# Sliding-window attention beside a long convolution on one core: logits and softmax in two halves, paired 64-row tails, and a fixed VectorE order at the end

## Chip, core and metric

The kernel runs on one core of a Trainium2 chip. The metric is the device time of one execution in microseconds (us); less is better. TensorE multiplies, VectorE and ScalarE work elementwise, GpSimd builds tables, and the queues of SyncE (SP), ScalarE and GpSimd start transfers, which 16 DMA engines carry out.

## What is computed

Two blocks that do not depend on each other, written side by side into the output (S = 2048, D = 576, bfloat16):

```python
# block A: 32 heads of 18, each token looks at itself and at 7 tokens before it, two apart
q, k, v = split(x @ wqkv)
idx = pos[:, None] - 2 * arange(8)[None, :]           # mask: idx >= 0
logits = einsum("bhsd,bhswd->bhsw", q, k[idx]) * 18 ** -0.5
a = einsum("bhsw,bhswd->bhsd", softmax(where(mask, logits, -1e9)), v[idx]) @ wo
# block B: a 4-tap shift convolution, a gate, and a causal convolution over the whole sequence
kv = (sum of k_pad[:, t:t + S] * shift_k[:, 3 - t] over 4 taps) * v_B
y = irfft(rfft(kv, 2 S) * rfft(ssm_k, 2 S))[:S]       # per channel
b = q_B * (y + kv * ssm_D)
out = concatenate([a, b], -1)
```

## The kernel before

*Block A.* x is transposed into xT by 80 TensorE transposes (L146); the rows 512 to 576 of the contraction are held as a fifth block of 128 rows whose first half is zero. From xT come q and k (qk_step L248, qk_half_step L260; steps of 128 channels by 1,024 tokens) and v (v_step L235). wv is held with its columns permuted from (head, d) to (d, head); permute_wv (L309) does this on ScalarE, after a load into a scratch area. logit_step, one for each of the 8 window positions, multiplies q and shifted k on VectorE (L395, L403) and adds the 18 products of a head by a matmul with a 0/1 matrix (L398, L407), into Lsb. Only when all 8 are there can the softmax begin: softmax_a (maximum, subtraction, exponential) and softmax_b (sum, reciprocal, product), each in two halves of columns, then at_step transposes the weights. pv_step(tp), for two of the 16 values of t mod 16, forms P = v x weights on VectorE (L547), adds over the window by matmuls with the identity (L556), and multiplies by wo (L569).

*Block B.* The long convolution is a two-step Fourier transform by matmuls, with its intermediate results in DRAM: x_step (shift convolution of kv_step on VectorE, L342 to L348, then the first transform s1_chunk, L279) writes Dx; k_step (transposes L293, then s1_chunk) writes Dk. kh_step does the second transform s2 (L454) of the filter into Khat; g_step does s2 for x, multiplies the spectra on VectorE (L491 to L494), does the inverse of the second transform (L500) and writes Dy; y_step does the last transform (L586), multiplies by q_B (L587) and stores.

*Order.* The program is written as a sequence of steps, and `run(a, b)` mixes two lists of them in proportion: q and k steps with x and k steps; logits with kh and v steps; then softmax, v 12 to 15, the copy of v's window rows (halo), g 0 and 1; then pv steps with g and y steps. A scheduler places the instructions of a step on the engines by priority, which follows the written order; each engine then runs its own queue in order. Two pools of two PSUM buffers each, pa (psA) and pb (psB), pass results to ScalarE and VectorE, and the input and Wt loads, the stores and the intermediate transfers go through SP's queue.

Of the kernel before, what the change touches and what calls it, by code (L numbers as in the profile page):

```python
# [18 lines left out]
def kernel(  # L19
# [114 lines left out]
    nc.gpsimd.memset(wq[0:64, 4, :], 0.0)  # L134
    nc.gpsimd.memset(wv[0:64, 4, :], 0.0)


    for qtr in range(4):
# [100 lines left out]
    def wcols(kb, comp, ct):  # L239
        return wq[:, kb, comp * D + 128 * ct:comp * D + min(128 * ct + 128, D)]  # L240

    def qk_step(comp, ct, jp):
        pad = PADL if comp else 0
        ps = psa()
        for u in range(2):
            j = 2 * jp + u
            for kb in range(5):
                nc.tensor.matmul(ps[:, u, :], wcols(kb, comp, ct), xT[:, kb, 512 * j:512 * j + 512],  # L248
                                 start=(kb == 0), stop=(kb == 4))
        dest = (k2 if comp else q2)[ct // 2][:, ct % 2, pad + 1024 * jp:pad + 1024 * jp + 1024]  # L250
# [376 lines left out]
```

## Time and profile before

| | |
|---|---|
| median of 3 timed runs | 293.98 us (292.49 to 295.75) |
| the profiled execution | 296.45 us, of which the span of the trace 294.6 us |
| busy: TensorE, weight loads | 241.2 us (82%), 152.6 us |
| busy: VectorE, ScalarE, GpSimd | 201.3 us (68%), 167.5 us (57%), 25.9 us (9%) |
| moved by DMA | 52.37 MB, mean 178 GB/s |
| mean granted TensorE clock | 0.905 of 2.4 GHz |

Busy times are of one execution. Weight loads run beside matmuls. A group's row gives its busy time, the mean of one instruction, and the idle time of the engine just before it with what ended that idle time. The chain of waits is followed back from the last instruction; each piece says what ran or what was waited for. A TensorE instruction's own duration holds its latency too, so the pitch of a row of matmuls is read from a piece of the chain, length over count.

### The profile page before, as it was taken

What the parts mean: (1) busy time and instruction counts of PE and PEld (TensorE: products, weight loads), DVE (VectorE), ACT (ScalarE), POOL (GpSimd) and SP (SyncE); (2) the same over time, 40 slices, a digit from 0 to 9 for tenths busy, and PEclk for the clock granted to TensorE, in tenths of its full rate; (3) what the DMA queues carried; (4) which work ended last, traced back from release to release, by engine and by line L of the source; (5) the groups of instructions that cost most, each with busy time, mean ns of one, the idle gap of its engine ahead of it and who ended that gap; (6) DMA issues with size and microseconds to landing.
All of it is one profiled execution on the core that took longest, in us unless ns stands there. A gap on an engine that the chain in (4) does not pass through costs nothing.

```text
span 294.6 us, 5101 instructions
## 1 busy us (share of the span) xinstructions
PE 241.2 (82%) x2129; PEld 152.6 (52%) x2129; DVE 201.3 (68%) x188; ACT 167.5 (57%) x242; POOL 25.9 (9%) x60
## 2 busy tenths in 40 slices
PE   1579269999997779999999455379999999997993
PEld 1464024555543336565547233168676766766782
DVE  3750895898771149899977991685879669694531
ACT  2422656668868662877877957323576585550311
POOL 8200000000000000000000845000000000012200
PEclk9999859999999778999999857558999999998999
DMA  7999623595555556653344198820442432559982
GB/s 232 360 323 305 234 77 144 178 285 163 160 162 160 160 160 184 222 148 94 103 148 145 40 278 221 283 82 0 123 146 110 149 127 94 184 154 309 328 255 80
DMA packets 42594, 52.37 MB, mean 178 GB/s; under 512 B 2174, under 2 KB 36686, under 8 KB 42445
## 3 DMA queue, kind: packets, MB, share of 16 engines
q1 hardware_dynamic: 39644, 47.04, 50.4%
q0 software_dynamic: 1264, 3.17, 4.3%
q10 hardware_dynamic: 1664, 1.84, 1.9%
q8 instruction: 16, 0.26, 0.3%
q14 instruction: 6, 0.05, 0.0%
HBM read 31.11 MB, written 18.87 MB: 170 GB/s over the span
## 4 chain that ended last, share of the span: by engine, by line
PE 50%; ACT 17%; DMA 16%; DVE 11%; issue 5%; SPq 1%; DVEq 0%; ACTq 0%
PE psA L248 9%; PE psA L235 7%; PE psB L279 6%; PE psA L556 5%; PE psB L454 5%; PE psA L569 5%; DMA out_dram<-m 4%; DMA xnat<-in_A_x_dram 4%; ACT Xc L457 4%; DMA Dy<-Y 4%; DMA k<-in_A_wqkv_dram 4%; PE psB L293 3%; PE psA L398 3%; ACT Y L503 3%; ACT vst L283 3%
## 5 line engine op out<-in xcount | busy, mean ns | idle before, releaser
L248 PE MATMUL psA<-xT,wq 128*128 128x512 bf16 x160 | 42.7, 407 | 8.7 <-ACT q L251 8.1
L556 PE MATMUL psA<-ident,P 128*128 128x128 bf16 (+1 forms) x640 | 46.2, 231 | 1.5 <-DVE P L547 1.4
L556 PEld LDWEIGHTS <-P 128*128 128x128 bf16 (+1 forms) x640 | 40.9, 107 | 8.4 <-issue 4.6
L547 DVE TENSOR_TENSOR P<-vX,at 128x4608 bf16<-128x4608 bf16 x16 | 40.1, 2550 | 4.3 <-PE psA L556 4.3
L283 ACT ACTIVATE vst<-psB 128x768 bf16<-128x768 f32 x48 | 36.3, 814 | 9.1 <-PE psB L279 8.0
L395 DVE TENSOR_TENSOR prod<-q,k 128x4096 bf16<-128x4096 bf16 x16 | 36.1, 2284 | 0.8 <-PE psA L398 0.6
L248 PEld LDWEIGHTS <-wq 128*128 128x128 bf16 x160 | 16.2, 103 | 27.8 <-issue 14.1
L454 PE MATMUL psB<-Wt,W 128*64 128x288 bf16 x256 | 28.0, 312 | 1.5 <-ACT Y L503 0.6
L560 ACT ACTIVATE xT<-psA 128x1024 bf16<-128x1024 f32 x8 | 8.2, 1024 | 34.8 <-PE psA L556 34.8
L500 PE MATMUL psB<-m,IAt 64*128 64x288 bf16 x128 | 14.9, 320 | 14.2 <-DVE m L493 7.6
L235 PE MATMUL psA<-wv,xT 128*128 128x288 bf16 x160 | 25.3, 294 | 0.3 <-ACT vX L237 0.3
L491 DVE TENSOR_TENSOR m<-Xc,Khat 128x2304 bf16<-128x2304 bf16 x8 | 10.8, 1356 | 18.6 <-ACT Xc L457 18.6
L503 ACT ACTIVATE Y<-psB 128x576 bf16<-128x576 f32 x32 | 18.9, 650 | 7.4 <-PE psB L500 6.1
L296 DVE COPY kTt<-psB 128x1152 bf16<-128x1152 bf16 x8 | 6.1, 758 | 24.0 <-PE psB L293 23.9
L569 PE MATMUL psA<-wv,xT 128*128 128x288 bf16 x160 | 22.3, 287 | 0.0
L235 PEld LDWEIGHTS <-xT 128*128 128x128 bf16 x160 | 18.8, 147 | 6.8 <-issue 6.8
L539 POOL DMA_DIRECT2D wv<-in_A_wo_dram x18 | 8.9, 501 | 151.7 <-PE psA L235 146.2
L457 ACT ACTIVATE Khat<-psB 128x576 bf16<-128x576 f32 x32 | 19.5, 653 | 3.4 <-PE psB L454 3.1
L587 DVE TENSOR_TENSOR m<-psB,Lsb 128x576 bf16<-128x576 f32 x16 | 11.4, 752 | 14.6 <-DMA out_dram<-m 8.2
L457 ACT ACTIVATE Xc<-psB 128x576 bf16<-128x576 f32 x32 | 19.6, 651 | 1.3 <-PE psB L454 1.1
L454 PEld LDWEIGHTS <-W 128*64 128x64 bf16 x256 | 12.7, 112 | 13.5 <-issue 11.9
L146 PE MATMUL psA<-ident,xnat 128*128 128x128 bf16 x80 | 9.5, 310 | 11.1 <-DMA xnat<-in_A_x_dram 10.0
(116 smaller groups left out, 331.2 us busy)
## 6 DMA issues: line engine op xcount, KB each, us to landing
Dx<-vst SPq DMA_DIRECT2D x16, 288.0 KB, 3.0
Dk<-vst SPq DMA_DIRECT2D x16, 288.0 KB, 3.0
Wt<-Dk SPq DMA_DIRECT2D x8, 576.0 KB, 3.8
Wt<-Dx SPq DMA_DIRECT2D x8, 576.0 KB, 3.9
Dy<-Y SPq DMA_DIRECT2D x8, 576.0 KB, 3.0
Wt<-Dy SPq DMA_DIRECT2D x8, 576.0 KB, 6.0
kX<-in_B_k_dram SPq DMA_DIRECT2D x3, 1008.0 KB, 5.2
vt<-in_B_v_dram SPq DMA_DIRECT2D x4, 576.0 KB, 8.3
```

The source lines that it names most:

```text
L235: nc.tensor.matmul(ps[:, di, 0:288], xTt[:, kb, t2, :], wv[:, kb, d0:d1], start=(kb == 0), stop=(kb == 4))
L248: nc.tensor.matmul(ps[:, u, :], wcols(kb, comp, ct), xT[:, kb, 512 * j:512 * j + 512], start=(kb == 0), stop=(kb == 4))
L279: nc.tensor.matmul(ps[:, ri, 0:384], T1[:, ri, :], sf[:, 384 * ch:384 * ch + 384], start=True, stop=not extra)
L283: nc.scalar.activation(vst[:, :, 384 * ch:384 * ch + 384], ps[:, :, 0:384], ACT.Copy)
L395: nc.vector.tensor_tensor(prod[:], q2[ct // 2][:], k2[ct // 2][:, :, sh:sh + S], ALU.mult)
L454: nc.tensor.matmul(ps[64 * hp:64 * hp + 64, im, 0:HD], W2[:, im, 8 * g + 2 * prl + hp].rearrange("p l f -> p (l f)"), Wt[:, 2 * prl + hp, ...
L457: nc.scalar.activation(dst[:, :, prl, :], ps[:, :, 0:HD], ACT.Copy, scale=scale)
L500: nc.tensor.matmul(ps[:, hp, 0:HD], IAt[64 * hp:64 * hp + 64, zi, 4 * g + prl, :], m1[64 * hp:64 * hp + 64, zi, prl, :], start=(zi == 0), ...
L503: nc.scalar.activation(Y[:, 2 * prl:2 * prl + 2, :], ps[:, :, 0:HD], ACT.Copy)
L547: nc.vector.tensor_tensor(P[:].rearrange("p w (d h) -> p w d h", h=H), vs, at[:, :, t2, :].unsqueeze(2).to_broadcast([128, W, DH, H]), ALU ...
L556: nc.tensor.matmul(oacc[0:csz, ci, 128 * u:128 * u + 128], Ps[u][:, wi, 128 * ct:128 * ct + csz], ident[:], start=(ci % 2 == 0 and u == 0 ...
L569: nc.tensor.matmul(pso[:, di, 0:288], oT[:, ct, t2, :], wot[:, ct, d0:d1], start=(ct == 0), stop=(ct == 4))
```

## The change

1. **Halves of t mod 16.** Logits are formed for t mod 16 below 8 first (all 8 window positions), then for the rest: `logit_unit(hf, wi)`. Each has its own tile Lh[hf], its own softmax and its own transposed weights ath[hf]. Half 0's softmax stands among the logit units of half 1. Each product has half the columns of before, in runs of 8 elements.
2. **Moved work.** q and k steps are by 512 tokens and begin when the first quarter of x is transposed. The first transforms of x alone stand beside them; those of the filter, all v steps and the halo (now in four parts) stand beside the logits; kh steps 4 to 7 stand in the last stage. The table transposes (ia_tables) come early.
3. **Loads.** x, weights, k and v of block B all go through SP, x 0 first, then the q and k weights, x 1, the first k and v block, x 2, x 3. B_shift_k is loaded once as one row and spread over the partitions by a matmul. wv is loaded without permutation; v's eviction permutes.
4. **Paired tails.** The rows 512 to 576 of xT, of the weights and of oT are held twice (both halves of 128 partitions), and their 64-row matmuls are issued in pairs for the two halves of the array; the last 64 columns of P are summed for two t in two column halves.
5. **Fixed VectorE order in the last stage.** `pin` makes each P product and each spectral product follow the one before it in the written order; `plan` says which k, g and y steps go with which tp. The second transform of g + 1 is issued ahead of the product of g.
6. **Memory.** Pools on the other sides, slabs of `cv` shared by several uses (tA: convolution, Lh, q_B; vt: v_B, ath; tB: convolution, sums, Y; wide: k_B and products).

```diff
-            for kb in range(5):
-                nc.tensor.matmul(ps[:, di, 0:288], xTt[:, kb, t2, :], wv[:, kb, d0:d1],
-                                 start=(kb == 0), stop=(kb == 4))
-        nc.scalar.activation(vX[:, 14 + t2, :].rearrange("p (i d) -> p i d", i=2), ps[:, :, 0:288], ACT.Copy)
+            for kb in range(4):
+                nc.tensor.matmul(ps[:, di, 0:288], xTt[:, kb, t2, :], wv[:, kb, d0:d1], start=(kb == 0), stop=False)
+        for di, (d0, d1) in enumerate(DCH):
+            r = slice(64 * di, 64 * di + 64)
+            nc.tensor.matmul(ps[:, di, 0:288], xTt[r, 4, t2, :], wv[r, 4, d0:d1], start=False, stop=True,
+                             tile_position=(64 * di, 0))
+        nc.scalar.activation(vX[:, 14 + t2, :].rearrange("p (d i h) -> p d i h", i=2, h=16),
+                             ps[:, :, 0:288].rearrange("p i (h d) -> p d i h", d=DH), ACT.Copy)
...
+                prod = wide().rearrange("p (c t) -> p c t", c=2)[:, :, 0:1024].rearrange("p c (a b) -> p c a b", b=8)
+                qv = q2[h][:].rearrange("p c (a b) -> p c a b", b=NT)[:, :, :, 8 * hf:8 * hf + 8]
+                kv = k2[h][:, :, sh:sh + S].rearrange("p c (a b) -> p c a b", b=NT)[:, :, :, 8 * hf:8 * hf + 8]
+                nc.vector.tensor_tensor(prod, qv, kv, ALU.mult)
+                for c in range(2):
+                    for j in range(4):
+                        nc.tensor.matmul(psw[32 * j:32 * j + 32, u, 0:256].rearrange("p (a b) -> p a b", b=2),
+                                         Eh[:, 2 * h + c, :], prod[:, c, :, 2 * j:2 * j + 2],
+                                         start=(h == 0 and c == 0), stop=False, tile_position=(0, 32 * j))
...
+    units = [logit_unit(hf, wi) for hf in range(2) for wi in range(W)]
+    for n, un in enumerate(units):
+        run(un, fill[3 * n:3 * n + 3] + vh[n * 20 // 13:(n + 1) * 20 // 13])
+        with tc.high_priority():
+            if n == 9:
+                softmax_a(0)
+            if n == 10:
+                softmax_b(0)
+            if n == 12:
+                at_step(0)
...
+        if n >= 12:
+            kh_step(n - 12)
+    with tc.high_priority():
+        softmax_a(1)
+        softmax_b(1)
+        at_step(1)
...
+    plan = [(("k4", "g0"), ("k5", "g1")), (("k6", "g2"),), (("k7", "g3"), ("g4",)), (("g5",), ("y0",)),
+            (("g6",), ("y1",), ("y2",)), (("g7",), ("y3",)), (("y4",), ("y5",)), (("y6",), ("y7",))]
+    g_spec(0)
+    for tp in range(8):
+        pv_mul(tp)
...
+        for n, i in enumerate(ng):
+            if i + 1 < 8:
+                g_spec(i + 1)
+            if n == 0:
+                pv_sum(tp)
+            g_prod(i)
+            if n == 0 and tp > 0:
+                pv_out(tp - 1)
+            g_inv(i)
```

Three places show how instructions move. The first is ScalarE's queue at the second and third q and k steps, where before the copies that permute wv stand (k_1 there is the scratch area that the weights were loaded into). Before:

```order
L251 ACTIVATE q_0_286<-psA 128x1024
L251 ACTIVATE k_0_288<-psA 128x1024
L309 ACTIVATE wv<-k_1_289 128x576 x4
L309 ACTIVATE wv<-k_1_289 64x576
L251 ACTIVATE q_0_286<-psA 128x1024
```

Now, the same queue from the last piece of B_shift_k (sk) through the first quarter's q and k steps to the second quarter of xT:

```order
L361 ACTIVATE sk<-psB 128x4x64
L283 ACTIVATE q_0_87<-psA 128x2x512
L283 ACTIVATE k_0_89<-psA 128x2x512
L283 ACTIVATE q_1_88<-psA 128x2x512
L283 ACTIVATE k_1_90<-psA 128x2x512
L181 ACTIVATE xT<-psA 128x2x512
L283 ACTIVATE q_0_87<-psA 128x2x512
```

The four copies of wv and the fifth of 64 rows are gone from between the q and k evictions, and nothing of the v weights stands in their place.

The second place is VectorE's queue at the second half's softmax (before: the only one). Lsb are the logits, mx the maxima and sums, m a spectral product. Before, from the subtraction of the maximum on:

```order
L422 TENSOR_TENSOR Lsb<-Lsb,mx 128x8x256 x2
L491 TENSOR_TENSOR m_1688<-Xc,Khat 128x2304
L492 TENSOR_TENSOR m_1689<-Xc,Khat 128x2304
L493 TENSOR_TENSOR m_1688<-m_1688,m_1689 128x1152
L494 TENSOR_TENSOR m_1688<-m_1688,m_1689 128x1152
L428 TENSOR_TENSOR mx_1771<-Lsb 128x1024
L428 TENSOR_TENSOR mx_1781<-Lsb 128x1024
L429 TENSOR_TENSOR mx_1771<-mx_1771 128x512
L429 TENSOR_TENSOR mx_1781<-mx_1781 128x512
L431 TENSOR_TENSOR ssum<-mx_1771 128x256
L431 TENSOR_TENSOR ssum<-mx_1781 128x256
L433 RECIPROCAL rec<-ssum 128x256 x2
```

Now, where tA is half 1's logits, tB its maxima and sums, and vt the transposed weights ath:

```order
L493 TENSOR_TENSOR tA<-tA,tB 128x2048
L640 TENSOR_TENSOR P<-vX,vt 128x4608
L500 TENSOR_TENSOR tB<-tA 128x1024
L640 TENSOR_TENSOR P<-vX,vt 128x4608
L501 TENSOR_TENSOR tB<-tB 128x512
L568 TENSOR_TENSOR m_2131<-Xc,Kc 128x2304
L503 TENSOR_TENSOR tB<-tB 128x256
L569 TENSOR_TENSOR sk<-Xc,Kc 128x2304
L505 RECIPROCAL tB<-tB 128x256
L570 TENSOR_TENSOR m_2131<-m_2131,sk 128x1152
L507 CAST tB<-tB 128x256
L571 TENSOR_TENSOR m_2131<-m_2131,sk 128x1152
```

Before, a single spectral product stood inside the softmax and every P behind it; now the first two P, which need half 0 alone, stand between the two passes of half 1's softmax, and the first spectral product is threaded through the second. TensorE's transposes of half 1 stand ahead of all sums over P in its queue.

The third place is VectorE's queue in the last stage, with the waits, where output steps (L690, into m) and the last spectral product (L568 to L571) alternate:

```order
L640 TENSOR_TENSOR P<-vX,vt 128x4608
L640 TENSOR_TENSOR P<-vX,vt 128x4608 [waits PE_49]
L690 TENSOR_TENSOR m_3049<-psB,tA 128x576 [waits DMAHW7_49,DMASW6_49,PE_49]
L690 TENSOR_TENSOR m_3049<-psB,tA 128x576 [waits PE_49]
L690 TENSOR_TENSOR m_3067<-psB,tA 128x576 [waits DMASW7_49,DVE_49,PE_49]
L690 TENSOR_TENSOR m_3067<-psB,tA 128x576 [waits PE_49]
L568 TENSOR_TENSOR m_3169<-Xc,Kc 128x2304 [waits DMAHW3_49,DVE_49,Activation_49]
L569 TENSOR_TENSOR sk<-Xc,Kc 128x2304
```

Before, all output steps stood behind the last spectral product, five of them in a row behind the fifteenth P; now they are spread among products and P from tp 3 on, and both kinds share the two buffers m, so the last spectral product waits for a store (DMAHW).

## Rows read from the trace of the kernel before

**Rows 1.** Busy time by stage: PE, PEld, DVE, ACT, POOL (instructions); PEclk, DMA share, GB/s.
```profile
0.00:21.20 21.20, 9.53 (x81) 8.41 (x82) 11.76 (x33) 7.03 (x7) 8.75 (x32) 1.00 0.93 306
21.20:39.30 18.10, 10.06 (x40) 4.22 (x40) 8.78 (x7) 9.01 (x9) 0.00 (x0) 0.86 0.74 233
39.30:110.00 70.70, 65.38 (x343) 31.66 (x343) 43.32 (x37) 49.42 (x63) 0.00 (x0) 0.91 0.55 172
110.00:158.50 48.50, 47.69 (x496) 27.73 (x494) 42.88 (x34) 32.66 (x56) 0.00 (x0) 0.97 0.48 147
158.50:190.40 31.90, 17.19 (x135) 11.53 (x134) 23.42 (x30) 21.84 (x33) 13.44 (x23) 0.69 0.72 206
190.40:202.10 11.70, 9.81 (x90) 8.15 (x90) 7.44 (x4) 2.92 (x5) 0.00 (x0) 0.53 0.13 53
202.10:259.80 57.70, 54.65 (x672) 39.16 (x669) 47.02 (x31) 37.07 (x61) 0.00 (x0) 1.00 0.36 119
259.80:294.60 34.80, 26.91 (x282) 21.75 (x280) 16.70 (x19) 7.50 (x12) 3.74 (x5) 0.93 0.78 238
sum 294.60, PE 241.21 PEld 152.61 DVE 201.32 ACT 167.47 POOL 25.93; mean PE 30.15 PEld 19.08 DVE 25.16 ACT 20.93 POOL 3.24
```

**Rows 2.** Chain of waits: start us, length us, what, xcount.
```profile
21.05 11.16 DMA k<-in_A_wqkv_dram
...
52.15 2.26 PE psA L248 x10
...
92.17 1.17 PE psB L293 x10
...
129.76 2.12 PE psA L235 x16
...
132.45 0.61 PE psB L454 x8
...
133.46 0.57 PE psA L398 x8
...
195.43 7.11 PE psA L556 x72
...
207.78 2.80 PE psA L556 x48
```

**Rows 3.** VectorE groups by shape: busy us, mean ns | idle before, releasers.
```profile
L547 DVE TENSOR_TENSOR P<-vX,at 128x4608 bf16<-128x4608 bf16 x16 | 40.1, 2550 | 4.3 <-PE psA L556 4.3
...
L395 DVE TENSOR_TENSOR prod<-q,k 128x4096 bf16<-128x4096 bf16 x16 | 36.1, 2284 | 0.8 <-PE psA L398 0.6
...
L347 DVE TENSOR_TENSOR tA<-tA,tB 128x2304 bf16<-128x2304 bf16 x12 | 16.3, 1356 | 0.3
...
L587 DVE TENSOR_TENSOR m<-psB,Lsb 128x576 bf16<-128x576 f32 x16 | 11.4, 752 | 14.6 <-DMA out_dram<-m 8.2 <-PE psB L586 6.3
...
L491 DVE TENSOR_TENSOR m<-Xc,Khat 128x2304 bf16<-128x2304 bf16 x8 | 10.8, 1356 | 18.6 <-ACT Xc L457 18.6
...
L493 DVE TENSOR_TENSOR m<-m,m 128x1152 bf16<-128x1152 bf16 x8 | 6.1, 758 | 0.3
...
L433 DVE RECIPROCAL rec<-ssum 128x256 f32<-128x256 f32 x2 | 3.4, 1718 | 0.0
...
L422 DVE TENSOR_TENSOR Lsb<-Lsb,mx 128x2048 bf16<-128x2048 bf16 x2 | 2.4, 1218 | 0.0
```

**Rows 4.** Groups by shape on TensorE (L248) and ScalarE.
```profile
L248 PE MATMUL psA<-xT,wq 128*128 128x512 bf16 x160 | 42.7, 407 | 8.7 <-ACT q L251 8.1 <-ACT xT L149 0.6
...
L283 ACT ACTIVATE vst<-psB 128x768 bf16<-128x768 f32 x48 | 36.3, 814 | 9.1 <-PE psB L279 8.0 <-ACT kh L269 0.8
...
L237 ACT ACTIVATE vX<-psA 128x576 bf16<-128x576 f32 x16 | 10.4, 651 | 6.6 <-PE psA L235 6.6
...
L309 ACT ACTIVATE wv<-k 128x576 bf16<-128x576 bf16 x4 | 4.7, 1254 | 4.1 <-DMA k<-in_A_wqkv_dram 4.1
```

**Rows 5.** DMA issues: what, queue, count, size of one, us to landing.
```profile
out_dram<-m SPq DMA_DIRECT2D x8, 288.0 KB, 5.2
```

More of the change, by code (lines that the diff above doesn't have):

```diff
@@ L133, with x_tr @@
     nc.vector.tensor_copy(ident[:], ident_f[:])
[L134 to L138 removed]
+    def x_tr(qtr):
+        nc.vector.tensor_copy(xns[qtr][:, :, D:640], xns[qtr][:, :, 512:D])
         for kp in range(3):
@@ L256, in qk_half_step @@
         for j in range(2):
-            for kb in range(5):
+            for kb in range(4):
                 for hh in range(2):
@@ new lines, in qk_steps, with sk_step @@
+    def qk_steps(j):
+        return [lambda comp=comp, cp=cp: qk_step(comp, cp, j) for cp in range(2) for comp in range(2)]
+    skb = slab("sk", 1, (4, D), "skb")
+    ones1 = tw.tile([1, 128], BF16, name="ones1")
+    nc.gpsimd.memset(ones1[:], 1.0)
+    def sk_step():
+        for i in range(3):
+            n = 256 if i < 2 else 64
+            ps = psb()
+            for u in range(2 if i < 2 else 1):
+                m = 512 if i < 2 else 256
+                nc.tensor.matmul(ps[:, u, 0:m], ones1[:], shr[:, 1024 * i + 512 * u:1024 * i + 512 * u + m],
+                                 start=True, stop=True)
+            nc.scalar.activation(skb[:, :, 256 * i:256 * i + n],
+                                 ps[:].rearrange("p u (d j) -> p j (u d)", j=4)[:, :, 0:n], ACT.Copy)
@@ new lines, in x_part @@
+    def x_part(c2, ch):
+        if c2 % 2 == 0 and ch == 0:
+            kvt[0] = kv_conv(c2 // 2)
+        s1_part(kvt[0][:, 2 * (c2 % 2):2 * (c2 % 2) + 2, :], "x", c2, ch, Dx, False)
+    x_tr(0)
+    sk_step()
+    for f in qk_steps(0):
+        f()
+    ia_tables()
+    x_tr(1)
+    kvl[1] = load_kv(1)
+    nc.sync.dma_start(wv[:, 0:4, :], A_wqkv[0:512, 2 * D:3 * D].rearrange("(kb p) a -> p kb a", p=128))
+    for p0 in (0, 64):
+        nc.sync.dma_start(wv[p0:p0 + 64, 4, :], A_wqkv[512:576, 2 * D:3 * D])
@@ new lines, with k_tr @@
+    for f in qk_steps(1):
+        f()
+    x_tr(2)
+    x_tr(3)
+    tw.release()
+    xin.release()
+    kpre = pool("kpre", 1, "right")
+    knats = []
+    for db in range(5):
+        n = 128 if db < 4 else 64
+        kn = kpre.tile([128, S], BF16, name=f"knat{db}")
+        nc.sync.dma_start(kn[0:n, :], B_ssm_k[128 * db:128 * db + n, :])
+        knats.append(kn)
+    nc.gpsimd.dma_start(Db[:], B_ssm_D.partition_broadcast(128))
+    ktt = {}
+    def k_tr(c2):
+        ktt[c2] = kpre.tile([128, 2, D], BF16, name="kTt", bufs=3)
+        ptr = pb.tile([128, 2, 1024], BF16, name="psB")
+        for u in range(2):
+            for db in range(5):
+                n = 128 if db < 4 else 64
+                nc.tensor.transpose(ptr[:, u, 128 * db:128 * db + n],
+                                    knats[db][0:n, :].rearrange("p (a b) -> p b a", b=NT)[:, 2 * c2 + u, :],
+                                    ident[0:n, 0:n])
+        nc.vector.tensor_copy(ktt[c2][:], ptr[:, :, 0:D])
@@ new lines, in k_part, with xs, ks, ld @@
+    def k_part(c2, ch):
+        if ch == 0 and c2 == 0:
+            k_tr(0)
+            k_tr(1)
+        if ch == 0 and c2 + 2 < 8:
+            k_tr(c2 + 2)
+        s1_part(ktt[c2], "k", c2, ch, Dk, True)
+    def xs(c2s):
+        return [lambda c2=c2, ch=ch: x_part(c2, ch) for c2 in c2s for ch in range(3)]
+    def ks(c2s):
+        return [lambda c2=c2, ch=ch: k_part(c2, ch) for c2 in c2s for ch in range(3)]
+    def ld(c):
+        def f():
+            kvl[c] = load_kv(c)
+        return f
```

532 lines of the change are left out of this document (265 added, 267 removed).

## Prediction

> **What bounds the kernel now.** I read the busy windows first: one row per stage, with each engine's busy time and TensorE's granted clock [rows 1]. The reader should see three kinds of stretch. Up to 21.2 us the DMA engines are the limit (share 0.93) and TensorE works 9.5 us. From 39.3 to 158.5 and from 202.1 to 259.8 TensorE is busy over 90% of the time. In between lie two holes. From 21.2 to 39.3 TensorE works 10.1 of 18.1 us: the chain of waits runs through an 11.16 us load of the v weights [rows 2], behind which ScalarE reorders them in four copies of 1.25 us and a fifth of 64 rows [rows 4]; the next eviction of q stands behind these copies in ScalarE's queue, and the group of the q and k matmuls lost 8.1 us for it [rows 4]. From 158.5 to 202.1 everything waits for the softmax: TensorE is busy 27 of 43.6 us at a clock of 0.69 and then 0.53, so the first 72 sums over P take 7.11 us where 48 later ones take 2.80 (0.099 and 0.058 us each) [rows 1, 2]. At the end, from 259.8, TensorE is busy 26.9 of 34.8 us, and VectorE waits 8.2 us for output stores before it may refill their buffers [rows 3].
>
> No engine is near its sum: VectorE has 201.3 us of work, ScalarE 167.5 [rows 1]. TensorE's 241.2 are partly stretched by the clock. At the pitches of undisturbed chain pieces (128x512: 0.226; 128x288: 0.1325; 128x128 sums: 0.058 [rows 2]) I get about 208 us. So the question is whether the change closes the holes, and at what price in work.
>
> **Prices of the edits.** *Paired tails.* Eight matmuls of the two-at-a-time form take 0.61 us [rows 2], where four times 0.1325 is 0.53; eight of the four-at-a-time form with 512 columns take 0.57, where twice 0.226 is 0.45. So members of a group do run beside each other, and entering and leaving such a group costs 0.08 to 0.12 us; I use 0.1. A pair of 512-column tails then costs 0.33 instead of 0.45 (16 pairs, -2.0 us), a v pair 0.23 instead of 0.265 (16, -0.5), four tails of the output product 0.365 instead of 0.53 (8, -1.3), sixteen 64-row sums 0.57 instead of 0.93 (8, -2.9): -6.7 us together. Row-halved pairs of 512 columns are not in the trace; between no overlap (+1.6 us) and full overlap without a switch (-3.6) I take the rows of the nearest paired form. [...] *Logits by halves.* Before, 16 groups of eight (0.57) and 8 of eight with 256 columns (0.35 by the same rule): 11.9 us. After, 32 groups at 0.35 and 16 with 128 columns at 0.23: 14.9, +3.0. *B_shift_k by matmul*: five of 512 columns, +1.1. TensorE's sum thus hardly moves (-2.6).
>
> *VectorE.* A product of 4,096 elements takes 2.284 us, one of 2,048 takes 1.218 [rows 3]: 32 x 1.218 - 36.1 = +2.9. The small products go from 5.5 to 16 x 0.43 = +1.4 (0.51 ns per element, from the 1,152 and 2,048 rows). Four new copies of 256 elements, +1.2; the copy of skb goes, -1.4. Sum +4.1. The new products read runs of 8 elements, which the trace lacks: bounds are 1.218 and, at the 1 ns per element of the PSUM product (0.752 for 576 [rows 3]), 2.3. I take the lower end, since P's product, in runs of 32 with a broadcast operand, keeps 0.55 ns per element.
>
> *ScalarE.* The permutation (6.0) goes into v's eviction, which costs between 0.65 as now and 1.25 as the permuting copy did [rows 4]: 0 to +9.6 us over 16. I take the upper end, its nearest row. Sixteen steps share the logits stage with TensorE, which hides them (below).
>
> So no work disappears. The gain must come from where the waits go.
>
> **Stage 1, to the end of the shift convolutions.** x leaves SP's queue ahead of everything, and the first k, v pair stands behind the q and k weights and a second x block: 0.6 + 1.5 + 0.6 + 1.6 = 4.3 MB, at 306 GB/s [rows 1] 14 us plus some 2 to issue. New on VectorE: the copy that doubles x's tail stands ahead of the identity and the tables, so these wait for x; I allow 2 us, hidden since the k, v data come later anyway. The convolutions start near 17 us; the load and copy of skb that they waited for are gone. VectorE then runs 32 operations of 1.356 us (43.4 [rows 3]), x and table copies (some 8), two early products (2.4): end near 71. TensorE has 128 x 0.226 + 16 x 0.33 for q and k, 80 + 34 transposes at 0.117 [rows 2], some 11 of others: 59 us from about 6, with some 6 of waits for x and its copies, and ends beside it. Its last six column blocks of Dx wait for convolution 3: ScalarE evicts them at 0.81 each [rows 4], so stage 2 is under way at 75.
>
> **Stage 2, logits.** TensorE: v 16 x 1.29 = 20.6; the transforms of B_ssm_k, moved here, 8 x 1.17 [rows 2] + 24 x 0.35 = 17.8; logits 14.9; four steps of kh 16 x 0.365 = 5.8; transposes 1.9: 61.0 us. VectorE: 30 products and 16 small ones 43.4, kTt 8 x 0.76 = 6.1, softmax of half 0 some 7.5 (reciprocal 1.7, two passes of 1.2, the rest short [rows 3]): 57. ScalarE: 24 x 0.81 + 16 x 1.25 + 8 x 0.6 + 16 x 0.65 + 5 = 60. Three engines within 4 us of each other. In the old logits stage 496 matmuls worth 45.5 us by the same pitches (v 16.7, kh 13.1, logits 11.9, table transposes 3.8) filled 48.5 us [rows 1], 0.94; 61.0 / 0.94 = 64.9. The last logits lie 1.5 before TensorE's end: half 1's softmax starts at 75 + 64.9 - 1.5 = 138.
>
> **Stage 3.** VectorE alternates half 1's softmax with P for t 0 and 1 and the first spectral product: 2.8 + 2.55 + 0.7 + 2.55 + 0.4 + 4.2 + 0.4 + 1.7 + 0.8 + 0.3 + 1.2 = 17 us. The transposes of half 1 stand in TensorE's queue ahead of all of P's sums, though the first sums need half 0 alone: this is the added wait, TensorE has only four second-transform steps (16 evictions of 0.65, some 10 us) to fill the 17, and the third P of the three buffers stalls behind it. Its clock will be low then: transposes 1.9, sums 4.3, slowed by 2, so at +25 the regular part begins. Left for TensorE: 7 x 4.3 sums, 8 x 2.5 output products, 8 second-transform steps (six of x, two of the filter) at 1.46, 7.5 inverse steps at 1.2, 8 y steps at 1.06 = 79 us; for VectorE 13 x 2.55 + 6 x 4.2 + 16 x 0.75 = 70. The old regular part did five rounds worth 80 x 0.058 + 20 x 0.1325 + 1.46 + 1.2 = 9.97 each in 57.7 us [rows 1], 0.865, because each spectral step waited for its own eviction: VectorE lost 18.6 us to that [rows 3]. Now the spectrum is issued a group ahead, so I take 0.93: 85 us. One new wait: the last spectral product shares two buffers with the output stage and needs the store of y 1, 5.2 us to landing [rows 5], with 1.5 of other work beside it: 3.7 us on VectorE, in whose fixed order the next P stands behind; TensorE's lead in sums covers it. After the last matmul two evictions of 0.65 [rows 4] and a store, some 5. So 138 + 25 + 85 + 5 = 253 us of span, against 294.6 [rows 1]. The profiled execution took 296.45, 1.85 more than its span; the median of the runs is 293.98, 0.8% lower. 254.9 less 0.8% is 253.
>
> **Rivals.** *The engines wait in turns* (20%). Two buffers each of psA and psB serve every stage, and in stage 2 ScalarE, TensorE and VectorE are equally loaded. With stage 2 at 0.85 and stage 3 at the old 0.865: +7 and +7, 267 us. For: the old stage from 39.3 to 110 had TensorE busy 65 of 70.7 us with ScalarE at 49. Against: the look-ahead. *VectorE's order holds* (11%): TensorE finds room in every gap, and VectorE sets the end: 71 + 57 + 88 + 4 + 12 of tail plus 3 = 235. *The 8-element runs lose half rate* (8%): 32 x 1.07 + 16 x 0.26 = 38 us on VectorE in stage 2, of which TensorE's 65 against VectorE's 57 hides some 7: 253 + 31 = 284. *TensorE stays at its lower clock* (6%): after the stretch in which it was busy 17.2 of 31.9 us the clock was 0.53 [rows 1], and each us of work costs two there. By the clocks of [rows 1] the old execution had some 56 us at 1.2 GHz, the lower level; my sum leaves it about 15. If the many short waits hold it low in stages 2 and 3, 44 us must be lost to end above 297: from 88 us at the lower level it is slower. Against: from 202.1 the clock was 1.00 with waits of 14% of the time. Of this case I count 2% within 1%.
>
> **Numbers.** Likeliest 253 (55%; its own range 244 to 262). 238 to 277 leaves out the half-rate case, the clock case and half of VectorE's: 19%. About 1% is what a measurement can tell from no change: faster 0.94, same 0.02, slower 0.04.
>
> **What would show it.** Right: no TensorE hole over 5 us between 21 and 135; the first product of the convolutions before 20 us; last convolution at 68 to 75; half 1's softmax at 132 to 145, with P's products inside it; one TensorE wait of 5 to 8 us for half 1's weights; regular rounds near 10.5 us; the halved products at 1.2 us, v's eviction near 1.25, a pair of tails near 0.33. Wrong: halved products near 2.3; half 1's softmax after 150; a clock under 0.85 past 160 us; rounds of 11.3 as before; VectorE waiting for stores more than 8 us.

## The result, and the profile after

The changed kernel takes 270.16 us (median of 4 runs, 269.15 to 270.82), the kernel before took 294.67 beside it: ratio 0.917, 95% interval 0.911 to 0.924. The forecast was 253 with a range of 238 to 277: direction right, time inside the range, 17 us above the likeliest and outside the 244 to 262 that the likeliest case had for itself. Executions of the kernel before spread by 2% with the granted clock (in one set of seven from 290.5 us at 0.93 to 296.0 us at 0.90), so a gain of a few us is read from the ratio and its interval. The profiled execution took 270.18 us, its span is 268.5.

Busy time by stage of the changed kernel (columns as in [rows 1]):

```profile
0.00:16.10 16.10, 10.32 (x39) 4.13 (x40) 7.70 (x29) 7.08 (x8) 7.48 (x31) 1.00 0.90 296
16.10:35.00 18.90, 18.68 (x133) 9.07 (x132) 18.43 (x22) 8.04 (x8) 0.00 (x0) 1.00 0.71 250
35.00:68.70 33.70, 30.68 (x191) 13.57 (x189) 31.72 (x27) 24.24 (x31) 0.00 (x0) 1.00 0.68 228
68.70:110.00 41.30, 40.56 (x354) 23.68 (x355) 23.67 (x28) 25.64 (x37) 0.00 (x0) 1.00 0.38 115
110.00:147.20 37.20, 34.45 (x408) 18.79 (x407) 30.90 (x38) 25.45 (x37) 9.35 (x19) 1.00 0.64 187
147.20:163.00 15.80, 9.79 (x80) 5.09 (x79) 15.66 (x18) 13.65 (x21) 1.28 (x2) 0.89 0.72 217
163.00:205.00 42.00, 38.18 (x482) 24.87 (x483) 32.44 (x25) 32.94 (x54) 0.76 (x1) 0.96 0.43 148
205.00:241.00 36.00, 32.18 (x405) 23.55 (x403) 29.13 (x23) 20.43 (x35) 2.25 (x3) 1.00 0.65 205
241.00:253.00 12.00, 9.35 (x123) 7.50 (x120) 8.90 (x8) 2.38 (x4) 1.49 (x2) 1.00 0.91 284
253.00:268.50 15.50, 10.77 (x129) 8.29 (x126) 4.00 (x6) 3.58 (x6) 0.75 (x1) 0.91 0.56 182
```

Against [rows 1], the hole from 21 to 39 us is gone (TensorE is busy 18.7 of 18.9 us), and that at the softmax shrank: from 147.2 to 163 TensorE works 9.8 of 15.8 us at a clock of 0.89, where it fell to 0.69 and 0.53. The groups that answer to [rows 3, 4] (halved product, v's eviction, output product):

```profile
L466 DVE TENSOR_TENSOR wide<-q,k 128x2048 bf16<-128x2048 bf16 x32 | 38.9, 1228 | 7.4 <-PE psA L469 7.3
...
L266 ACT ACTIVATE vX<-psA 128x576 bf16<-128x576 f32 x16 | 10.4, 650 | 12.4 <-PE psA L264 12.4
...
L690 DVE TENSOR_TENSOR m<-psB,tA 128x576 bf16<-128x576 f32 x16 | 11.7, 755 | 13.8 <-PE psB L689 10.0 <-DMA out_dram<-m 3.7
```

Both prices that the prediction held to be uncertain came out at their cheap ends: 1,228 ns for a product in runs of 8, and 650 ns for the eviction that reorders, where the upper end of 1.25 us was taken.

The convolutions, as rows of VectorE in order of time (start us, length us): the first product and the last of them, before and then after.

```profile
31.82 1.36 DVE L342 TENSOR_TENSOR tA<-kX,skb 128x2304 bf16<-128x2304 bf16 x1
...
85.47 1.35 DVE L348 TENSOR_TENSOR tA<-tA,vt 128x2304 bf16<-128x2304 bf16 x1
```

```profile
16.11 1.35 DVE L370 TENSOR_TENSOR tA<-wide,sk 128x2304 bf16<-128x2304 bf16 x1
...
67.34 1.36 DVE L376 TENSOR_TENSOR tA<-tA,vt 128x2304 bf16<-128x2304 bf16 x1
```

They start 15.7 and end 18.1 us earlier. The softmax (its first operation, the mask) in the kernel before, and half 1's in the changed one with the first P:

```profile
156.58 0.18 DVE L416 TENSOR_TENSOR Lsb<-Lsb,maskb 128x32 bf16<-128x32 bf16 x1 [3.40 <-ACT Lsb L411]
```

```profile
147.09 0.17 DVE L488 TENSOR_TENSOR tA<-tA,maskb 128x16 bf16<-128x16 bf16 x1 [2.54 <-ACT tA L482]
...
149.95 2.55 DVE L640 TENSOR_TENSOR P<-vX,vt 128x4608 bf16<-128x4608 bf16 x1
```

Half 1's softmax begins at 147.1 (before, the only one at 156.6), so 9.5 of the 26.1 us of span lie ahead of the softmax and 16.6 behind its start.

TensorE among the logits, in order of time (the next row's start less a row's own is its pitch), before and then after:

```profile
128.75 0.40 PE L407 MATMUL psA<-prodh,Eh 128*32 128x256 bf16 x8
129.08 0.68 PE L454 MATMUL psB<-Wt,W 128*64 128x288 bf16 x7
```

```profile
110.72 0.63 PE L469 MATMUL psA<-wide,Eh 128*32 128x256 bf16 x8
111.29 0.34 PE L336 MATMUL psB<-kTt,T 128*128 128x384 bf16 x1
...
112.55 0.40 PE L478 MATMUL psA<-prodh,Eh 128*32 128x128 bf16 x8
112.88 0.50 PE L336 MATMUL psB<-kTt,T 128*128 128x384 bf16 x2
```

Eight logit matmuls of 256 columns take 0.57 us and eight of 128 columns 0.33. The prediction had 0.35 and 0.23. The group with 512 columns took 0.57 before [rows 2]: half the columns now cost as much. The small product's group of 256 columns took 0.33 before, so the forecast 0.35 was right for the old way of reading. Before, the matmul picked 4 neighbours of 16 elements of the product; now it picks 2 of 8. The chain of waits at the end (start us, length us, what) holds two transfers:

```profile
230.17 2.44 DMA out_dram<-m
...
244.14 7.75 DMA Wt<-Dy
...
263.85 0.65 ACT stageA L673
```

### The profile page after: what moved, and what is told of

Same layout as the page of the kernel before. It is cut to its first block, busy times and chain, and to the rows that moved or that the text cites. A ratio compares the mean times of both kernels' runs of the same rounds, so it can differ in the third digit from the quotient of the medians.

```text
span 268.5 us, 5519 instructions
## 1 busy us (share of the span) xinstructions
PE 235.0 (88%) x2326; PEld 138.5 (52%) x2326; DVE 202.6 (75%) x216; ACT 163.4 (61%) x236; POOL 23.4 (9%) x59
## 4 chain that ended last, share of the span: by engine, by line
PE 56%; DVE 22%; ACT 11%; issue 4%; DMA 4%; POOL 2%; SPq 0%; ACTq 0%; DVEq 0%; POOLq 0%
PE psA L278 7%; PE psA L469 6%; PE psA L650 6%; PE psA L261 6%; PE psB L336 6%; PE psB L526 5%; DVE P L640 5%; PE psB L419 3%; PE psA L666 3%; DVE tA L375 3%; DMA Wt<-Dy 3%; DVE tB L370 2%; DVE m L568 2%; DVE sk L569 2%; ACT Xc L529 2%
## 5 line engine op out<-in xcount | busy, mean ns | idle before, releaser
L341 ACT ACTIVATE vst<-psB 128x768 bf16<-128x768 f32 x48 | 37.0, 812 | 12.7 <-PE psB L336 11.3
L466 DVE TENSOR_TENSOR wide<-q,k 128x2048 bf16<-128x2048 bf16 x32 | 38.9, 1228 | 7.4 <-PE psA L469 7.3
L640 DVE TENSOR_TENSOR P<-vX,vt 128x4608 bf16<-128x4608 bf16 x16 | 40.5, 2554 | 2.9 <-PE psA L656 2.8
L650 PE MATMUL psA<-ident,P 128*128 128x128 bf16 x512 | 37.7, 221 | 3.6 <-DVE P L640 2.9
L650 PEld LDWEIGHTS <-P 128*128 128x128 bf16 x512 | 30.0, 98 | 14.0 <-issue 8.6
L469 PE MATMUL psA<-wide,Eh 128*32 128x256 bf16 x256 | 21.7, 400 | 1.1 <-ACT vX L266 1.1
L690 DVE TENSOR_TENSOR m<-psB,tA 128x576 bf16<-128x576 f32 x16 | 11.7, 755 | 13.8 <-PE psB L689 10.0
L584 ACT ACTIVATE tB<-psB 128x576 bf16<-128x576 f32 x32 | 19.4, 658 | 4.1 <-PE psB L581 3.0
L529 ACT ACTIVATE Kc<-psB 128x576 bf16<-128x576 f32 x32 | 20.0, 650 | 2.2 <-PE psB L526 1.7
L261 PE MATMUL psA<-wv,xT 128*128 128x288 bf16 x128 | 19.9, 292 | 0.6 <-ACT vX L266 0.6
L666 PE MATMUL psA<-wv,xT 128*128 128x288 bf16 x128 | 17.1, 286 | 2.0 <-ACT xT L652 2.0
L568 DVE TENSOR_TENSOR m<-Xc,Kc 128x2304 bf16<-128x2304 bf16 x8 | 10.8, 1356 | 8.3 <-ACT Xc L529 7.3
```

Of the source, the lines that this page charges most:

```text
L341: nc.scalar.activation(vst[:, :, 384 * ch:384 * ch + 384], ps[:, :, 0:384], ACT.Copy)
L466: nc.vector.tensor_tensor(prod, qv, kv, ALU.mult)
L469: nc.tensor.matmul(psw[32 * j:32 * j + 32, u, 0:256].rearrange("p (a b) -> p a b", b=2), Eh[:, 2 * h + c, :], prod[:, c, :, 2 * j:2 * j + ...
L529: nc.scalar.activation(dst[:, :, prl, :], ps[:, :, 0:HD], ACT.Copy, scale=scale)
L568: pin(nc.vector.tensor_tensor(m1[:], Xc[:], Kc[:, 0].unsqueeze(1).to_broadcast([128, 2, 4, HD]), ALU.mult))
L584: nc.scalar.activation(Y[:, 2 * prl:2 * prl + 2, :], ps[:, :, 0:HD], ACT.Copy)
```

## Experiments

Each run is compared with the kernel before on the same chip; the changed kernel's ratio to it is 0.917 (0.911 to 0.924).

**1. Why a logit group costs more than its price.** Edit of the changed kernel (the small product likewise):

```diff
-  Eh[:, 2 * h + c, :], prod[:, c, :, 2 * j:2 * j + 2],
+  Eh[:, 2 * h + c, :], prod[:, c, 32 * j:32 * j + 32, :].rearrange("p a (k b) -> p (a k) b", b=2),
```

> The changed kernel with one difference: the matmuls of the logits read 256 (or 128) neighbouring elements of the product, where they picked 2 of every 8 before. The number of columns, the products, the weights and all waits stay; what is added up belongs to other tokens, so the logits are others. Theory A (TensorE reads runs of 2 elements at half its rate): the group of eight with 256 columns falls from 0.56 to 0.35 us, the one with 128 from 0.33 to 0.22; 32 x 0.21 + 16 x 0.11 = 8.5 us less TensorE work in the stage in which it was busy 70.4 of 73.0 us, so half 1's softmax starts near 139 instead of 147 and the time is 262 to 265. Theory B (the group costs 0.56 for its entry, its exit and its many short matmuls, and the stage is lost to engines that wait in turns): groups stay at 0.5 or above, 269 to 271.

263.0 us, ratio 0.893 (0.884 to 0.902). TensorE in order of time:

```profile
104.91 0.29 PE L478 MATMUL psA<-prodh,Eh 128*32 128x128 bf16 x8
105.13 0.66 PE L336 MATMUL psB<-kTt,T 128*128 128x384 bf16 x3
...
107.07 0.40 PE L469 MATMUL psA<-wide,Eh 128*32 128x256 bf16 x8
107.40 0.34 PE L336 MATMUL psB<-kTt,T 128*128 128x384 bf16 x1
```

The groups fall to 0.33 and 0.22 us, the prices of the prediction, and half 1's softmax starts earlier:

```profile
139.71 0.17 DVE L488 TENSOR_TENSOR tA<-tA,maskb 128x16 bf16<-128x16 bf16 x1 [1.50 <-ACT tA L482]
```

Theory A holds: nothing but the spacing of what TensorE reads was changed. From 128 to 256 columns a group grows by 0.11 us here and by 0.24 in the changed kernel, so a column costs about twice as much there. 7.2 of the missing 17 us are this. Two elements of each 16 bytes made a group of 256 columns take 0.57 us for the 0.33 of 256 neighbours; four of each 32 bytes, in the kernel before, took 0.33 as well.

**2. The same by VectorE.** The product is written by pairs, in pieces of 2 elements, so that TensorE reads 256 neighbours:

```diff
-  nc.vector.tensor_tensor(prod, qv, kv, ALU.mult)
+  nc.vector.tensor_tensor(prod.rearrange("p j a b -> p a j b"), qv.rearrange("p a (j b) -> p a j b", b=2),
+                          kv.rearrange("p a (j b) -> p a j b", b=2), ALU.mult)
...
-  Eh[:, 2 * h + c, :], prod[:, c, :, 2 * j:2 * j + 2],
+  Eh[:, 2 * h + c, :], prod[:, j, 129 * c:129 * c + 128, :],
```

> The whole computation, with VectorE writing the product sorted by pairs of t (runs of 2 elements at the output, where it read and wrote runs of 8), so that TensorE reads 256 neighbouring elements. Theory A: TensorE's groups at 0.35 and 0.22 us as in the run with long reads. If VectorE writes short runs at its old pace (1.23 us a product), 262 to 265. If it falls to the 1 ns per element of its PSUM products (0.755 us for 576), 2.06 us a product, 32 x 0.83 + 16 x 0.1 = 28 us more on VectorE, which had 52.0 of 73.0 us in the stage and becomes its bound at 80: 277 or so. Theory B: TensorE's groups unchanged, 270 with the old pace of VectorE.

276.98 us, ratio 0.942 (0.934 to 0.949). Groups of this run:

```profile
L471 DVE TENSOR_TENSOR wide<-q,k 128x2056 bf16<-128x2056 bf16 x32 | 61.9, 2005 | 2.2 <-PE psA L475 2.1
L475 PE MATMUL psA<-wide,Eh 128*32 128x256 bf16 x256 | 14.9, 297 | 9.6 <-DVE wide L471 9.2 <-ACT vX L267 0.4
```

TensorE's groups are cheaper again (297 ns in the mean for 400), but TensorE now waits 9.2 us for VectorE, whose product takes 2.0 us: the price is moved, not removed. The time is the 277 that the expectation gave for this case.

**3. Tokens stored by pairs from the load on.** x's rows are loaded, and xT, q and k laid out, as (pair of t mod 16, t / 16, parity). A shift is then an offset in rows of pairs, and both engines run over 256 neighbours:

```diff
-    q2 = [qk.tile([128, 2, S], BF16, name=f"q2_{i}") for i in range(2)]
-    k2 = [qk.tile([128, 2, PADL + S], BF16, name=f"k2_{i}") for i in range(2)]
+    q2 = [qk.tile([128, 2, 8, 256], BF16, name=f"q2_{i}") for i in range(2)]
+    k2 = [qk.tile([128, 2, 8, 258], BF16, name=f"k2_{i}") for i in range(2)]
...
+  for a, b, o, sl in parts:                 # two parts where the shift crosses a border
+      nc.vector.tensor_tensor(prod[:, :, a:b, :], q2[h][:, :, 4 * hf + a:4 * hf + b, :],
+                              k2[h][:, :, o + a:o + b, sl:sl + 256], ALU.mult)
```

> The whole computation with tokens stored by pairs of t mod 16 from the load of x on (x rows are loaded in that order, xT, q and k are laid out as pair, t / 16, parity), so that products and logit matmuls run over 256 neighbouring elements on both engines; a product whose shift crosses the border of its half is made in two pieces (18 more VectorE instructions, some 0.16 us each, 3 us). Theory A: groups at 0.33 and 0.22 us as with the long reads (263.0 there), products in all as before plus 3 us on VectorE, which has room: 262 to 266. Rival (the reordering costs elsewhere: x lands later by its eight loads for one, evictions of q and k in runs of 64 are slower): 266 to 271.

263.92 us, ratio 0.902 (0.896 to 0.909): the whole computation, faster than both kernels, and inside theory A's 262 to 266. The logit group's mean falls from 400 to 277 ns, and half 1's softmax starts at 141.8:

```profile
L476 PE MATMUL psA<-wide,Eh 128*32 128x256 bf16 x256 | 13.6, 277 | 2.3 <-ACT vX L270 1.1 <-DVE wide L472 0.6 <-ACT vt L526 0.6
```

**4. Half 0's softmax under the logits.** First try: the calls for half 0 moved behind the last logit unit.

> The changed kernel, but the softmax of half 0 and its transposes stand behind all the logits, beside those of half 1, instead of between the logit units. Theory H (the gain at the softmax comes from half 0's work lying under the logits): 7.6 us of VectorE and 1.9 to 3.2 us of ScalarE between the last logit and the first P, during which TensorE has only second-transform steps: the first sum over P starts 8 to 11 us later and the time is 277 to 281. Rival (TensorE's queue is full anyhow, the two halves only change who waits): 269 to 273.

269.11 us, ratio 0.915 (0.908 to 0.923). The scheduler lifted them back: VectorE's queue differs from the changed kernel's by the place of one small product, ScalarE's by that of two evictions of the transposed weights. So this says nothing on theory H, but is nearly a second measurement of the changed kernel, 0.4% from the first. Second try: the first operation of half 0's softmax tied behind the last small product on VectorE.

```diff
+        if hf == 0:
+            tc.add_manual_dep(i0.ins, chain2[0].ins.name,      # the first operation, the last small product
+                              mybir.DependencyInfo(mybir.DependencyClass.NoSync, mybir.DependencyReason.DATA), reason="order")
```

> In the run e3 the scheduler lifted half 0's softmax back among the logits (VectorE did its subtraction at 121 us), so the question is open. Here the first operation of half 0's softmax is tied behind the last small product of half 1 in VectorE's queue. Theory H (half 0's softmax under the logits is worth its VectorE time): 7.6 us of VectorE, 1.9 to 3.2 us of ScalarE, and the transposes with their evictions come between the last logit and the first P, which starts some 12 us after the last logit and not 3; 277 to 281. Rival (what else waits in that stretch, second-transform steps and their evictions, takes as long): 269 to 273.

277.66 us, ratio 0.950 (0.942 to 0.958). VectorE in order of time (the mask of half 0's softmax; then the first P), and the stage's window:

```profile
140.63 0.17 DVE L490 TENSOR_TENSOR tA<-tA,maskb 128x16 bf16<-128x16 bf16 x1
...
156.82 2.56 DVE L642 TENSOR_TENSOR P<-vX,vt 128x4608 bf16<-128x4608 bf16 x1 [1.18 <-ACT vt L524]
```

```profile
140.00:172.00 32.00, 19.77 (x190) 11.78 (x187) 27.27 (x33) 24.40 (x35) 5.32 (x11) 0.68 0.56 170
```

The first P starts at 156.8 instead of 149.95, TensorE works 19.8 of 32 us, and the granted clock is 0.68 as in [rows 1]. Theory H holds: hiding the first softmax, with its transposes, is worth 7.5 us by the medians and 9.6 by the ratios (0.950 for 0.917).

**5. The first hole alone.** The kernel before, with wv loaded into its place and the reorder in v's eviction:

```diff
-  permute_wv()
...
-  nc.scalar.activation(vX[:, 14 + t2, :].rearrange("p (i d) -> p i d", i=2), ps[:, :, 0:288], ACT.Copy)
+  nc.scalar.activation(vX[:, 14 + t2, :].rearrange("p (d i h) -> p d i h", i=2, h=16),
+                       ps[:, :, 0:288].rearrange("p i (h d) -> p d i h", d=DH), ACT.Copy)
```

> The kernel before, with one part of the change alone: wv is loaded straight into its place without the four copies and the fifth on ScalarE, and v's eviction reorders the columns. Theory L (the hole from 21 to 39 us comes from q's eviction standing behind copies that wait for wv's load): TensorE's 8.1 us wait behind q's eviction goes; 286 to 288 against 294. Rival (the loads of x, k and v set the stretch anyway, the convolutions end as late): 291 to 294. v's eviction stays at 0.65 us as in the changed kernel.

290.27 us, ratio 0.988 (0.979 to 0.996): between the two expectations. By the ratio that is 3.6 us, with an interval of 1 to 6: a small gain whose size is not settled. The stretch's window, what VectorE waits for, and the softmax:

```profile
21.20:39.30 18.10, 16.85 (x74) 7.45 (x75) 9.31 (x8) 7.16 (x7) 0.00 (x0) 1.00 0.64 217
```

```profile
29.85 1.36 DVE L326 COPY skb<-q 128x2304 bf16<-128x2304 bf16 x1 [9.62 <-DMA q<-in_B_shift_k_dram]
31.25 1.36 DVE L343 TENSOR_TENSOR tA<-kX,skb 128x2304 bf16<-128x2304 bf16 x1
...
151.64 0.18 DVE L416 TENSOR_TENSOR Lsb<-Lsb,maskb 128x32 bf16<-128x32 bf16 x1 [3.40 <-ACT Lsb L411]
```

TensorE's hole is filled (16.9 of 18.1 us, at a clock of 1.00 for 0.86), yet the convolutions still wait for B_shift_k and its copy, start at 31.25 and end at 83.7. The softmax starts 4.9 us earlier than before: in the traces the copies give about half of the 9.5 us ahead of it. What gives the other half, the earlier start of the convolutions or the work moved between the stages, no run separates.

**6. The convolutions, later.** The first k and v block loaded behind x 2, x 3 and the v weights:

```diff
-    kvl = {0: load_kv(0)}
     load_x(2)
     load_x(3)
+    nc.sync.dma_start(wv[:, 0:4, :], A_wqkv[0:512, 2 * D:3 * D].rearrange("(kb p) a -> p kb a", p=128))
...
+    kvl = {0: load_kv(0)}
```

> The changed kernel, with the first block of k and v loaded behind x 2, x 3 and the v weights instead of ahead of them (1.8 MB, some 6 us at the 296 GB/s of the first stretch). The first product of the convolutions starts at 22 instead of 16.1 us. Theory C (the chain of convolutions on VectorE, 52.6 us long, sets the end of the first stage, so its start was the gain there): everything behind comes 5 to 6 us later, 275 to 277. Rival (TensorE's q and k work, 59.7 us busy of 68.7, takes it up): 270 to 272.

270.0 us, ratio 0.919 (0.912 to 0.926).

```profile
20.41 1.36 DVE L373 TENSOR_TENSOR tA<-wide,sk 128x2304 bf16<-128x2304 bf16 x1 [3.56 <-DMA wide<-in_B_k_dram]
...
69.56 1.35 DVE L379 TENSOR_TENSOR tA<-tA,vt 128x2304 bf16<-128x2304 bf16 x1
```

The start slipped by 4.3 us, the end by 2.2, and half 1's softmax began at 147.05 as without it: a slip of this size is taken up, as the rival said, and theory C fails. A larger slip came unasked in experiment 9: there the convolutions end 10.3 us later than in experiment 3 (83.1 against 72.8), with the same logits, and the softmax starts 7.9 us later. This would fit a chain of convolutions that sets the end of the first stage once it is some us behind; but x's loads differ between those two runs as well, so it is not shown.

**7. Three waits of the last stage, one at a time.** The transposes of half 1's weights behind the sums of tp 0; the spectral steps earlier; tiles of their own for the output products:

```diff
-  at_step(1)                       # ahead of the last stage
+  at_step(1)                       # behind pv_sum(0)
```

> The changed kernel, with the sixteen transposes of half 1's weights behind the sums of tp 0 in TensorE's queue (they are used from tp 4 on). Theory W (the added wait costs): the sums over the first two P, 4.3 us of TensorE, move from 164 into the hole in which TensorE worked 9.8 of 15.8 us, and everything behind them, which TensorE bounds, comes 3 to 5 us earlier: 265 to 267. Rival V (VectorE, busy 24.7 of the 25.7 us to 172, bounds that stretch, so TensorE only waits elsewhere): 269 to 271.

```diff
-  (("g5",), ("y0",)), (("g6",), ("y1",), ("y2",)), (("g7",), ("y3",)), ...
+  (("g5",), ("g6",)), (("g7",), ("y0",)), (("y1",), ("y2",), ("y3",)), ...
```

> The changed kernel with another plan: the spectral steps g 6 and g 7 one and one tp earlier, y 0 to y 3 later (tp 4: y 0; tp 5: y 1, y 2, y 3; tp 6 and 7 as before). Theory T (the end waits for g 7: its product waits for a store, and the first load of Dy behind it lands at 252): the 7.75 us wait for Wt from Dy goes from the chain, TensorE's waits of 1.7 us for it and 3.2 us of missing work at 238 and 250 close: 266 to 268. Rival (TensorE's work sets the end and is only reordered): 269 to 271.

```diff
-  stage = b2.tile([128, 2, 4, HD], BF16, name="m1")[:, 0]
+  stage = b2.tile([128, 4, HD], BF16, name="ys")
```

> The changed kernel, with tiles of their own for the output products of block B, so that the last spectral product no longer waits for a store (2.44 us in the chain of waits). Theory S (the chain of the tail, store, product, Dy, Wt, y, sets the end): 1 to 2.5 us faster, 267.5 to 269. Rival (TensorE's lead in sums covers the wait, as predicted): 269.5 to 271.

They take 271.29 (ratio 0.928, 0.920 to 0.935), 270.97 (0.926, 0.918 to 0.934) and 268.39 us (0.914, 0.905 to 0.923): none differs from the changed kernel by what can be told apart. The third lies where theory S put it, but also within the interval of the changed kernel's ratio, so a gain of 1 to 2 us from it is neither shown nor excluded. Each wait went, and another stood in its place. In the first, the sums start at 152.2 instead of 164.0, but a later P waits 3.00 us for TensorE where it waited 2.17; in the second, the output products wait for q_B; in the third, the chain still holds the load of Dy:

```profile
182.37 2.56 DVE L639 TENSOR_TENSOR P<-vX,vt 128x4608 bf16<-128x4608 bf16 x1 [3.00 <-PE psA L655]
```

```profile
239.76 5.35 DMA tA<-in_B_q_dram
```

```profile
243.19 7.20 DMA Wt<-Dy
```

**8. Tails one by one.** Both 64-row tails of q, k and v in the same rows of the array, P's tails for one t after the other, the tails of the output product u by u:

```diff
-            r = slice(64 * u, 64 * u + 64)
+            r = slice(0, 64)
...
-                             tile_position=(64 * u, 0))
+                             tile_position=(0, 0))
...
-        for wi in range(W):
-            for u in range(2):
+        for u in range(2):
+            for wi in range(W):
...
-        for di, (d0, d1) in enumerate(DCH):
-            for u in range(2):
+        for u in range(2):
+            for di, (d0, d1) in enumerate(DCH):
```

> The changed kernel, with the 64-row tails issued one after the other: the two tails of q, k and v in the same rows of the array, the tails of P for one t after the other, those of the output product u by u. By the prices of the prediction: sums 8 x 0.36 = 2.9, output 1.0 to 1.3, v 0.5 us in the stages that TensorE bounds, q and k 16 x 0.13 = 2.1 beside the convolutions of VectorE. Theory M (the pairs are worth their TensorE time where TensorE bounds): 273.5 to 275. Rival (TensorE's waits of some 9 us in the last stage absorb them): 269.5 to 271.5.

272.2 us, ratio 0.928 (0.921 to 0.935): between the two, 2 us by the medians and 3 by the ratios, whose intervals overlap. TensorE in order of time, a pair of q or k and sixteen sums, in the changed kernel and then here:

```profile
41.92 0.39 PE L281 MATMUL psA<-xT,wq 64*128 64x512 bf16 x2
42.24 0.82 PE L336 MATMUL psB<-tA,T 128*128 128x384 bf16 x4
...
221.97 0.64 PE L656 MATMUL psA<-ident,P 128*64 128x128 bf16 x16
222.54 0.42 PE L581 MATMUL psB<-m,IAt 64*128 64x288 bf16 x4
```

```profile
41.58 0.60 PE L281 MATMUL psA<-xT,wq 64*128 64x512 bf16 x2
42.11 0.82 PE L336 MATMUL psB<-tA,T 128*128 128x384 bf16 x4
...
223.42 0.89 PE L656 MATMUL psA<-ident,P 128*64 128x128 bf16 x16
224.24 0.42 PE L581 MATMUL psB<-m,IAt 64*128 64x288 bf16 x4
```

A pair takes 0.32 against 0.53 us, sixteen sums 0.57 against 0.82. Four tails of the output product take 0.26 us in either order, so that part of the edit took no pair apart. TensorE's busy time rises by 4.5 us (239.5 for 235.0; experiment 6, with the same work, has 233.3).

**9. Pairs and own tiles together.** Experiment 3 with x in four transfers a quarter (to every second partition) for eight, part of them through ScalarE's queue, and the tiles of experiment 7.

> The tokens by pairs as in the run e9, with x loaded in four transfers a quarter instead of eight, half of them of the first two quarters through ScalarE's queue, and with the output tiles of the run e13. In e9 the convolutions started at 21.5 us against 16.1, and ended 4 us later than in the changed kernel. If the first convolution starts near 17 again: 260 to 262. If the loads still come late: 263 to 264.

272.14 us, ratio 0.926 (0.918 to 0.934): far outside both expectations. The logits keep their gain, but the loads lose it: the chain of waits holds 6.38 and 6.55 us for blocks of k, and the last convolution starts at 81.8:

```profile
49.47 6.38 DMA wide<-in_B_k_dram
```

```profile
81.76 1.35 DVE L382 TENSOR_TENSOR tA<-tA,vt 128x2304 bf16<-128x2304 bf16 x1
```

The `pin` ties were not run apart. Without them the scheduler puts some P, spectral and output products of the last stage elsewhere in VectorE's queue, so what the fixed order is worth is not shown.

## Why the prediction was right, and where 17 us went

*The mechanism.* Two holes, closed at little price in work: right, but for the price of the logits below. The second is shown by experiment 4 (7.5 us, and the clock). For the first the prediction named the v weights' copies as what cost TensorE 8.1 us; experiment 5 gives 4.9 us of the softmax's start and 3.6 us of time (1 to 6) for them. The convolutions' start came at 16.1 (forecast 17), their end at 68.7 (71), the first transposes of the filter at 73.5 (75). That the time fell inside 238 to 277 is in part luck: this range was stretched to hold the rival of engines waiting in turns, and the likeliest case's own range, 244 to 262, was missed by 8 us.

*Step that failed: the price of a logit group.* 0.35 and 0.23 us were got by scaling columns from rows in which TensorE read its data in wider runs; the groups took 0.57 and 0.33 (experiment 1). 32 x 0.22 + 16 x 0.10 = 8.6 us; half 1's softmax started 9.1 us late (147.1 for 138). The prediction asked what runs of 8 would cost VectorE (nothing) and not what runs of 2 would cost TensorE. The rival of engines waiting in turns came nearest in time (267), but not for its reason in stage 2: TensorE was busy 70.4 of 73.0 us there.

*Half 1's softmax to the regular part.* The terms of the sum to the last product of the softmax add up to 17.6, not 17; it took 16.0. The added wait was sized as 5 to 8 us of TensorE that delays all behind it; in experiment 7 taking it away gained nothing, which fits VectorE being busy 24.7 of 25.7 us there.

*Regular part.* 79 us of work at 0.93 gave 85; from 172.2 (147.1 + 25) to the last matmul it is 91.65, with TensorE busy 82.2. Work was short by 3.2: the sums over P, priced as one run, are cut by the scheduler into 46 pieces between other groups, and four of them take 0.33 us there where 4 x 0.058 = 0.23. An estimate from these: 39 more pieces than one for each of the 7 tp, at 0.1, is 3.9 us; the granted clock, 0.98 there, can have a part in the 3.2 as well. Waits are 9.5 us instead of 6. The overlap failed here: 79 / 91.65 is 0.86, the old 0.865 and not 0.93. That 0.865 was put down to waits for evictions, but TensorE was busy 54.65 of those 57.7 us [rows 1]: 3.05 us were waits, and 4.8 us work above the pitches. The issue ahead could take away waits alone. In experiment 7 none of three waits, taken away by itself, moved the time clearly; the rival of waiting in turns fits this stage better, with rounds of 11.2 to 12.3 us and one of 16.5 with two spectral steps (forecast 10.5, named as wrong at 11.3).

*The rest.* The store's wait for the last spectral product was 2.44 us (3.7); taking it away moved the median by 1.8 us, which is not clear of noise. v's eviction was sized 9.6 us too high on ScalarE, which was busy only 45.8 of 73.0 us among the logits. Paired tails: -6.7 us of TensorE was near (4.5 by experiment 8, its output product left paired), but only 2 to 3 of them are time. The step from the span to the median took off 0.8% that the changed kernel does not have: 1.7 us between span and time, and no difference to the median. In sum 9.1 + 6.65 - 0.35 on the span (the end took 4.65 us for 5), and 1.7 more, are the 17 us. Refuted: VectorE's order as the bound, half rate at runs of 8 (1,228 ns), and a lasting low clock (0.98 in the mean).

Open: how the 16.6 us behind the softmax's start divide beyond the 7.5 of experiment 4, and which part the clock has. In slices of half a us the two traces give the granted clock as 1.00 or 0.50, with few values between: 471 and 102 of 588 slices before, 516 and 17 of 537 after. By the mean clock of 0.982 some 10 us of the changed execution were at 0.50 (2 x 0.018 x 268.5), where the prediction had 56 before and 15 after. Its 1.2 GHz for this level is half of the 2.4 GHz given with the profile before; what the runs show for that scale is that at 1.00 the pitches of [rows 2] grow by 0.417 ns a column ((226 - 132.5) / (512 - 288)), 2.4 columns in a ns.

## What to carry over

When a tensor is cut in halves along its innermost order, ask of every reader what run it now reads, TensorE too; the price scaled by columns, 0.35 us for a group of 256, held here in runs of 4 and in one long run (0.33 each), and not in runs of 2 (0.57). The last stage, with TensorE busy 82 of 92 us, did not answer clearly to the removal of any one wait; a layout that spared TensorE work among the logits gained 6 to 7 us. Before a stage's share of busy time is read as waits, compare the busy time itself with the work that was priced. And test each cause of a hole by itself: filling TensorE's hole alone moved the softmax by 4.9 us, while starting the convolutions 4.3 us later in the changed kernel did not move it.

## What the runs showed of the hardware

- TensorE's moving operand in runs of 2 bfloat16 elements (16 bytes apart): groups of eight took 0.57 and 0.33 us for 256 and 128 columns in the changed kernel, against 0.33 and 0.22 in one long run (experiment 1); in runs of 4 elements (32 bytes apart) a group took 0.33 for 256 in the kernel before.
- VectorE's product of 2,056 elements with an output in runs of 2 took 2.0 us (experiment 2); with runs of 8 at all operands, 1.23 for 2,048 in the changed kernel.
- ScalarE's eviction of v took 651 ns in the kernel before, where it read PSUM in order [rows 4], and 650 in the changed one, where it read it permuted by (head, d); the copies that permuted wv, read from SBUF, took 1.25 us each [rows 4].
- Two 64-row tails of 512 columns took 0.32 us side by side in the changed kernel and 0.53 one after the other (experiment 8).
